# Four PSUM banks for scores and relu, three for maxima, and new matmul orders in an attention kernel

## The chip, the core and the metric

The kernel runs on one core of a Trainium2 chip. The metric is the device time of one execution in microseconds (us); the lower the better. TensorE (PE in the profile; PEld for its weight loads) does the matmuls, VectorE (DVE) and ScalarE (ACT) read their results from the eight banks of PSUM, GpSimd (POOL) and SyncE (SP) do small work and issue DMAs.

## The reference

One input `x` of 2048 rows and 576 columns goes through two attentions of 32 heads with head width 18, and a gate mixes the results. Attention A has keys and values of its own for each head; attention B shares one key and one value head.

```
q, k, v = x @ wqkv                      # A: 32 heads of 18
p = softmax(q k^T * 18**-0.5);  a = (p v) @ wo_A
q = x @ wq;  k = x @ wk;  v = x @ wv    # B: 32 query heads, one k and one v
p = softmax(q k^T * 18**-0.5);  b = (p v) @ wo_B
g = sigmoid((x * gate_w).sum(-1))
out = g * a + (1 - g) * b               # 2048 x 576, float32
```

## The kernel before

A first stage splits `x` and the weights into two parts each and projects them; queries and keys leave as two half-precision parts. Then 64 heads (32 of B, then 32 of A) run one after another, and a last stage finishes the output projection.

A head has 16 steps, one for each 128 keys. A step makes four score matmuls, `sA0` to `sA3` or `sB0` to `sB3` (`step_scores`): 128 keys against 512 queries each, from rows 0 to 55 of the array, into a bank of the pool `ps_s`. ScalarE turns each into exponentials (tile `pt`). Four matmuls with the values then add these to `acc`, a bank of its own (`step_pv`); they run side by side in four column groups of the array, for all 512 columns or for one half of 256.

The softmax needs the row maxima before its exponentials. They are found 22 steps (`LEAD`) ahead of the scores: `step_max` makes matmuls of 128 queries against 512 keys from rows 64 to 117, into a bank of the pool `ps_m`, and VectorE reduces each. In every first step of a pair, one reduction is saved: a matmul with the difference of the first two key blocks (operation `x`) goes through a relu on ScalarE into `xb`, and VectorE adds it to block 0 while it takes the maximum (`mA0`, tile `junk`); block 1 has no matmul of its own. So a pair of steps has eight exponentials and one relu on ScalarE, seven reductions on VectorE, and 16 matmuls `s`, `m` and `x`. Since `s` and `m` use different rows of the array, two of them can run at once.

TensorE takes its matmuls strictly in the written order, and one that waits for its bank holds those behind it. The loop over pairs of steps at the end of the program walks through a string for each pair, and this string is the order:

- `PLAIN` is the ordinary pair.
- `END` comes where a new head begins: the last values of the old head are added (`Q`), then `head_out` copies `acc` to `oe` on VectorE. `AFTER` is the pair behind it.
- `UNIT` is a pair with one unit of the output projection (`U`): 12 matmuls of 288 columns into one more bank of `ps_m`. `SEG` and `at_ends` place the units: one at each start of the heads 33 to 53, one in the middle of every second head from 32 to 52, and in heads 59 to 62 one in nearly every pair.
- `LEADS` and `FIRST` are the pairs before the scores begin and the first with them, `ALONE` those at the end that have no maxima any more.

In the strings, `P` and `Q` stand for the values of a whole step, `p` and `f`, `h` and `H` for the first and second half of one. `max_rows` closes the maxima of a head (once per head, on VectorE). `turn_mask`, `balance` and `shared_v` belong to the first stage; `out_proj` and `last_out` make the output.

Of the kernel before, what the change touches and what calls it, by code (L numbers as in the profile page):

```python
# [8 lines left out]
F32 = mybir.dt.float32  # L9
# [7 lines left out]
PSUM = bass.MemoryType.PSUM  # L17
# [32 lines left out]
def gated_mix_kernel(ctx: ExitStack, tc: tile.TileContext, xT, wall, wv, wo, out):  # L50
# [8 lines left out]
    dram = ctx.enter_context(tc.tile_pool(name="dram", bufs=1, space=DRAM))  # L59
    ps_s = ctx.enter_context(tc.tile_pool(name="ps_s", bufs=3, space=PSUM))  # L60
    ps_m = ctx.enter_context(tc.tile_pool(name="ps_m", bufs=4, space=PSUM))
    ps_o = ctx.enter_context(tc.tile_pool(name="ps_o", bufs=1, space=PSUM))
# [98 lines left out]
    def turn_mask():  # L161
        pt = ps_m.tile([P, 512], F32, name="pm")
        for g in range(4):
            nc.tensor.transpose(pt[:, MT * g:MT * g + MT], mask_r[:, g, :], ident[0:MT, 0:MT])
        nc.vector.tensor_copy(mask, pt[:, 0:4 * MT].rearrange("p (g m) -> p g m", m=MT))
# [28 lines left out]
    def balance(g):  # L194
# [9 lines left out]
        yield  # L204
        pt = ps_m.tile([P, 512], F32, name="pm")
        nc.tensor.transpose(pt[0:2, 0:P], r, ident)
# [5 lines left out]
        yield  # L212
        pb = ps_m.tile([P, 512], F32, name="pm")
        nc.tensor.matmul(pb[:, 0:2], two, dg, start=True, stop=True)
# [60 lines left out]
    def shared_v(c):  # L275
        st = ST.pop(c)
        pv = ps_m.tile([P, 512], F32, name="pm")
# [222 lines left out]

    def step_max(u, i, c, low=False):
# [11 lines left out]
        nc.tensor.matmul(pm, qs[u % 3][b:b + 54, i * P:(i + 1) * P], k, start=True, stop=True)  # L513
        if c == "x":
            MX["x", u, i] = lead.tile([P, 512], F32, name="xb", bufs=2)
            nc.scalar.activation(MX["x", u, i], pm, AF.Relu)  # L516
        elif c == 0 and ("x", u, i) in MX:
            junk = lead.tile([P, 512], BF16, name="junk", bufs=1)
            nc.vector.tensor_tensor_reduce(junk, pm, MX.pop(("x", u, i)), 1.0, -3e38, op0=OP.add, op1=OP.max,  # L519
                                           accum_out=MX[u][:, i, c:c + 1])  # L520
        else:
            nc.vector.tensor_reduce(MX[u][:, i, c:c + 1], pm, axis=AX.X, op=OP.max)  # L522
# [112 lines left out]
    WO = {}  # L635

    def prep_wo(t0, rows):
        nt = len(rows)
# [10 lines left out]
    def out_proj(t0, rows, first=False):  # L649
# [18 lines left out]
        for q in range(8):  # L668
# [3 lines left out]
            for s2 in range(2):  # L672
                st_ = 2 * q + s2
                for hf in range(2):
                    fp = ps_m.tile([P, 512], F32, name="pm")
                    n = 0
# [29 lines left out]
    def last_out():  # L706
# [6 lines left out]
        for j in range(4):  # L713
# [3 lines left out]
            dma(stk[36:54, cs], ol[32 * j:32 * j + 18, :])  # L717
        pt = ps_m.tile([P, 512], F32, name="pm")
        for c in range(4):
# [7 lines left out]
        for st_ in range(16):  # L727
            for hf in range(2):
                ps = ps_m.tile([P, 512], F32, name="pm")
                nc.tensor.matmul(ps[:, 0:288], stk[0:54, st_ * P:st_ * P + P],  # L730
# [60 lines left out]
    FIRST = "sA0 mA2 sA1 mA0 sA2 mA3 mA1 sA3 mB0 sB0 mB1 sB1 mB2 sB2 mB3 sB3 x"  # L791
    PLAIN = "sA0 mA2 sA1 mA0 sA2 mA3 P sA3 mB0 sB0 mB1 sB1 mB2 h sB2 mB3 sB3 x H"
    UNIT = "sA0 mA2 sA1 mA0 sA2 mA3 P sA3 mB0 sB0 mB1 sB1 mB2 U sB2 mB3 sB3 x Q"
    END = "sA0 mA2 sA1 mA3 sA2 mB0 P sA3 mB1 sB0 mA0 sB1 x Q sB2 mB2 sB3 mB3"
    AFTER = "sA0 mA2 p sA1 mA0 sA2 mA3 sA3 x f sB0 mB0 sB1 mB1 h sB2 mB2 sB3 mB3 H"
    ALONE = "sA0 sA1 P U sA2 sA3 U sB0 sB1 h U sB2 sB3 H U"
    LEADS = "V.A mA0 MA1 mA2 MA3 V.B mB0 MB1 mB2 MB3"
    order = None
    for T in range(-LEAD, NSTEP + 2, 2):
# [5 lines left out]
        if M >= 16 and M % 16 == 0 and M // 16 - 1 < NU:  # L805
            max_rows(M // 16 - 1)
        alone = M >= NSTEP
        units = sum(due(t, Tb, Tc, 32) for t in (T, T + 1) for _, _, _, Tb, Tc in SEG)
        order = LEADS if T < 0 else FIRST if T == 0 else ALONE if alone else UNIT if units else \
            END if T % 16 == 0 else AFTER if order is END else PLAIN  # L810
        for op in order.split():
# [8 lines left out]
            elif k in "mM":  # L820
                step_max(*divmod(M + second, 16), int(c), k == "M")
            elif k == "s":
# [10 lines left out]
        if slow and M % 16:  # L833
            for _ in range(2 if T > 1000 else 1):
                if slow:
                    try:
                        next(slow[0])
                    except StopIteration:
                        slow.pop(0)
    while slow:  # L840
        run(slow.pop(0))
# [38 lines left out]
```

## Time and profile before

| | |
|---|---|
| median of 3 runs | 2697.82 us (2697.22 to 2697.87) |
| the profiled execution | 2698.16 us, of which its instructions span 2696.4 us |
| TensorE matmuls busy | 2663.0 us (99%) |
| VectorE busy | 2429.9 us (90%) |
| ScalarE busy | 2389.8 us (89%) |
| mean granted TensorE clock | 0.996 |

Busy shares are averages over stages: the first 280 us or so are projection. Matmuls are pipelined, so a busy TensorE is not one at its peak. In the rows of the timeline, an instruction's start can lie before the end of the one ahead of it on its engine; the distance of two ends then tells the engine's rate.

### The profile page before, as it was taken

Reading aid. Unit: us, or ns where it says so; the run is one execution under the profiler, and the core shown is the slowest. Engines: PE = TensorE matmul, PEld = TensorE weight load, DVE = VectorE, ACT = ScalarE, POOL = GpSimd, SP = SyncE. Lnnn points to the kernel's source line nnn. Section 1 sums busy time; section 2 is a strip of 40 time slices with the busy share of each in tenths; the row PEclk is TensorE's granted clock in tenths of the full one; section 3 lists DMA queues with packets and bytes.
Section 4 is the critical chain, followed back from the end, with each engine's and each line's share of the span. In section 5 each row is a group of like instructions: output and inputs, shape, how many; then the busy total and the mean of one; then the engine's idle time right before and its main releaser. Section 6 shows DMA issues by size and latency. Waiting matters only on the chain.

```text
span 2696.4 us, 57946 instructions
## 1 busy us (share of the span) xinstructions
PE 2663.0 (99%) x22210; PEld 955.2 (35%) x22210; DVE 2429.9 (90%) x4616; ACT 2389.8 (89%) x4809; POOL 280.0 (10%) x520
## 2 busy tenths in 40 slices
PE   9999999999999999999999999999999999999999
PEld 6888322222222222222223333333333332223444
DVE  8347999999999999999999999999999999998865
ACT  4341899999999999999999999999999999998875
POOL 4740000002001100100110001000200011011000
PEclk9999999999999999999999999999999999999998
DMA  6332000011001100110132113112121212122212
GB/s 200 125 110 78 20 20 20 18 32 45 25 20 46 44 20 18 52 33 18 38 76 81 44 48 87 43 49 64 57 67 50 57 51 61 39 73 83 88 36 96
DMA packets 127089, 150.36 MB, mean 56 GB/s; under 512 B 55339, under 2 KB 94411, under 8 KB 125614
## 3 DMA queue, kind: packets, MB, share of 16 engines
q1 hardware_dynamic: 113628, 121.86, 16.0%
q0 software_dynamic: 7968, 19.23, 2.1%
q10 hardware_dynamic: 5216, 5.57, 0.6%
q8 instruction: 174, 2.85, 0.4%
q14 instruction: 103, 0.84, 0.1%
HBM read 90.89 MB, written 46.45 MB: 51 GB/s over the span
## 4 chain that ended last, share of the span: by engine, by line
ACT 51%; PE 40%; DVE 6%; DMA 1%; issue 1%; SPq 1%; DVEq 0%; ACTq 0%
ACT pt L557 45%; PE acc L563 14%; PE ps L550 12%; ACT xb L516 6%; PE pm L679 4%; DVE mx L522 3%; PE pm L243 3%; PE ps L243 3%; PE ps L292 2%; PE pm L513 2%; DVE oe L573 1%; SPq L56 1%; DVE junk L519 1%; DMA xs<-xT 1%; DVE oacc L733 0%
## 5 line engine op out<-in xcount | busy, mean ns | idle before, releaser
L557 ACT ACTIVATE pt<-ps 128x512 f32<-128x512 f32 x4052 | 2095.0, 639 | 69.2 <-PE pm L513 61.2
L522 DVE TENSOR_REDUCE mx<-pm 128x1 f32<-128x512 f32 x3096 | 1941.4, 682 | 89.2 <-PE pm L513 74.9
L550 PE MATMUL ps<-qs,ksb 56*128 56x512 f16 x2688 | 819.4, 380 | 10.6
L513 PE MATMUL pm<-ksb,qs 54*128 54x512 f16 x2364 | 739.7, 383 | 1.9 <-DVE mx L522 1.0
L563 PE MATMUL acc<-pt,vb 128*19 128x512 f32 (+1 forms) x6136 | 592.7, 458 | 1.9
L563 PE MATMUL acc<-pt,vg 128*19 128x256 f32 (+1 forms) x5664 | 579.5, 481 | 2.3 <-DVE oe L573 0.5
L513 PEld LDWEIGHTS <-qs 54*128 54x128 f16 x4096 | 329.9, 93 | 247.3 <-issue 197.1
L550 PE MATMUL ps<-qs,ksa 56*128 56x512 f16 x1364 | 404.4, 379 | 4.8 <-ACT pt L557 1.3
L550 PEld LDWEIGHTS <-ksb 56*128 56x128 f16 x2688 | 175.0, 94 | 623.0 <-issue 576.5
L513 PE MATMUL pm<-ksa,qs 54*128 54x512 f16 x1232 | 385.0, 382 | 0.6 <-ACT xb L516 0.4
L519 DVE CUSTOM_DVE_ANT_0 junk<-pm,xb 128x512 bf16<-128x512 f32 x500 | 340.4, 681 | 0.0
L516 ACT ACTIVATE xb<-pm 128x512 f32<-128x512 f32 x500 | 317.6, 635 | 0.0
L550 PEld LDWEIGHTS <-ksa 56*128 56x128 f16 x1408 | 89.3, 94 | 328.7 <-issue 298.5
L532 POOL TENSOR_SCALAR mt<-mt 128x32 f32<-128x32 f32 x64 | 18.5, 288 | 1612.8 <-DVE mt L530 1612.8
L563 PEld LDWEIGHTS acc<-pt,vb 128*19 128x19 f32 x6136 | 104.0, 97 | 225.6 <-issue 208.5
L563 PEld LDWEIGHTS acc<-pt,vg 128*19 128x19 f32 x5664 | 96.1, 97 | 222.9 <-issue 204.9
L513 PE MATMUL pm<-kdb,qs 54*128 54x512 f16 x372 | 141.7, 381 | 0.0
L573 DVE COPY oe<-acc 128x512 f32<-128x512 f32 x63 | 43.6, 692 | 30.0 <-PE acc L563 27.9
L295 ACT ACTIVATE vst<-ps 128x288 f32<-128x288 f32 x32 | 13.1, 411 | 62.1 <-PE ps L292 62.1
L251 ACT ACTIVATE ph<-ps,tv 128x512 f16<-128x512 f32 x29 | 19.8, 686 | 49.9 <-PE ps L243 34.3
L251 ACT ACTIVATE ph<-pm,tv 128x512 f16<-128x512 f32 x27 | 18.5, 687 | 48.2 <-PE pm L243 35.7
L257 DVE SCALAR_TENSOR_TENSOR pl<-pm,tv,ph 128x512 f16<-128x512 f32 x27 | 20.1, 749 | 37.9 <-ACT ph L251 24.9
(150 smaller groups left out, 1504.1 us busy)
## 6 DMA issues: line engine op xcount, KB each, us to landing
qs<-qkh SPq DMA_DIRECT2D x244, 72.0 KB
qs<-qkl SPq DMA_DIRECT2D x122, 72.0 KB
onh<-oh SPq DMA_DIRECT2D x32, 256.0 KB
onl<-ol SPq DMA_DIRECT2D x32, 256.0 KB
oih<-onh SPq DMA_DIRECT2D x16, 512.0 KB
oil<-onl SPq DMA_DIRECT2D x16, 512.0 KB
ot<-oe SPq DMA_DIRECT2D x220, 36.0 KB
R<-r_d SPq DMA_DIRECT2D x55, 144.0 KB
```

What stands on the lines that cost most here:

```text
L243: nc.tensor.matmul(fp[:, a0:b0], w[a][:kr, k, :], X[b][:kr, k, s0 + a0:s0 + b0], start=(n == 0), stop=(n == len(PROJ) - 1), skip_group_che ...
L251: nc.scalar.activation(h, fp, AF.Copy, scale=t)
L292: nc.tensor.matmul(fp[:, 0:288], X[b][:kr, k, st_ * P:(st_ + 1) * P], w[a][:kr, k, :], start=(n == 0), stop=(n == len(PROJ) - 1))
L513: nc.tensor.matmul(pm, qs[u % 3][b:b + 54, i * P:(i + 1) * P], k, start=True, stop=True)
L516: nc.scalar.activation(MX["x", u, i], pm, AF.Relu)
L519: nc.vector.tensor_tensor_reduce(junk, pm, MX.pop(("x", u, i)), 1.0, -3e38, op0=OP.add, op1=OP.max, accum_out=MX[u][:, i, c:c + 1])
L522: nc.vector.tensor_reduce(MX[u][:, i, c:c + 1], pm, axis=AX.X, op=OP.max)
L550: nc.tensor.matmul(ps, kst(u)[b:b + 56, i * P:(i + 1) * P], qs[u % 3][b:b + 56, c * 512:(c + 1) * 512], start=True, stop=True)
L557: nc.scalar.activation(pt, ps, AF.Exp, scale=SCALE / LIFT ** 2)
L563: nc.tensor.matmul(acc[32 * j:32 * j + 19, a:b], v_of(u, i), PT[u, i, j][:, a:b], start=(i == 0 and a == 0), stop=(i == 15), skip_group_ch ...
L573: nc.vector.tensor_copy(oe, acc)
L679: nc.tensor.matmul(fp[:, 0:288], o[b][:r, t, s2 * P:(s2 + 1) * P], w[a][:r, t, 288 * hf:288 * hf + 288], start=(n == 0), stop=(n == 3 * nt ...
```

## The change

Three things are done at once.

1. `ps_s` has four banks and `ps_m` three, where it was three and four. The matmul `x` that feeds the relu goes to `ps_s`, so that pool serves ScalarE alone in the main stage, and `ps_m` serves VectorE and the units.
2. The strings are new, and there are separate ones for a unit at a head's start (`UNIT_END`) and for the heads 59 on (`UNIT2`). `AFTER` now also follows a head's start with a unit.
3. Where `ps_m` had uses beside the maxima, they are moved: small transposes of the first stage go to parts of `acc`, each fourth maximum of `LEADS` to `ps_s`, and after the loop the output matmuls take turns over both pools (`seven`).

```diff
-    ps_s = ctx.enter_context(tc.tile_pool(name="ps_s", bufs=3, space=PSUM))
-    ps_m = ctx.enter_context(tc.tile_pool(name="ps_m", bufs=4, space=PSUM))
+    ps_s = ctx.enter_context(tc.tile_pool(name="ps_s", bufs=4, space=PSUM))
+    ps_m = ctx.enter_context(tc.tile_pool(name="ps_m", bufs=3, space=PSUM))
...
     def turn_mask():
-        pt = ps_m.tile([P, 512], F32, name="pm")
+        pt = acc[:, 192:256]
...
+    def other():
+        return ps_s.tile([P, 512], F32, name="ps")
+
+    def step_max(u, i, c, low=False, spare=False):
...
-        pm = ps_m.tile([P, 512], F32, name="pm")
+        pm = other() if c == "x" or spare else ps_m.tile([P, 512], F32, name="pm")
...
+    def seven():
+        L["tail"] += 1
+        return other() if L["tail"] % 7 < 4 else ps_m.tile([P, 512], F32, name="pm")
...
-    PLAIN = "sA0 mA2 sA1 mA0 sA2 mA3 P sA3 mB0 sB0 mB1 sB1 mB2 h sB2 mB3 sB3 x H"
+    PLAIN = "mB1 mB3 sA0 sA1 mA3 sA2 P mB2 sA3 x sB0 mA2 sB1 mB0 h sB2 mA0 H sB3"
...
+    UNIT_END = "mB3 sA0 mA2 sA1 mA3 sA2 P sA3 mB1 sB0 mB2 Q x sB1 mA0 sB2 mB0 sB3 U"
...
-        order = LEADS if T < 0 else FIRST if T == 0 else ALONE if alone else UNIT if units else \
-            END if T % 16 == 0 else AFTER if order is END else PLAIN
+        order = LEADS if T < 0 else FIRST if T == 0 else ALONE if alone else (UNIT2 if T >= SEG[1][3] else UNIT_END if T % 16 == 0 else UNIT) if units else \
+            END if T % 16 == 0 else AFTER if T % 16 == 2 and T > 2 else PLAIN
```

What the new strings do to TensorE's queue, at three places. The names: `ps` is a score (in the new kernel also `x`), `pm` a maximum, `acc` the values; `ksb` and `qs` are keys and queries, `kdb` the key difference; the numbers tell tiles apart. First the ordinary pair, from behind `H` to `P`, before:

```order
L550 LDWEIGHTS ksb_95
L550 MATMUL ps_8827<-qs1_93,ksb_95 128x512
L513 LDWEIGHTS qs2_94
L513 MATMUL pm_8831<-ksb_95,qs2_94 128x512
L550 LDWEIGHTS ksb_95
L550 MATMUL ps_8834<-qs1_93,ksb_95 128x512
L513 LDWEIGHTS qs2_94
L513 MATMUL pm_8838<-ksb_95,qs2_94 128x512
L550 LDWEIGHTS ksb_95
L550 MATMUL ps_8842<-qs1_93,ksb_95 128x512
L513 LDWEIGHTS qs2_94
L513 MATMUL pm_8846<-ksb_95,qs2_94 128x512
```

The same stretch of TensorE's queue after the change, from `mB1` to the last matmul ahead of `P`:

```order
L516 LDWEIGHTS qs2_94
L516 MATMUL pm_8788<-ksb_95,qs2_94 128x512
L516 LDWEIGHTS qs2_94
L516 MATMUL pm_8791<-ksb_95,qs2_94 128x512
L553 LDWEIGHTS ksb_95
L553 MATMUL ps_8794<-qs1_93,ksb_95 128x512
L553 LDWEIGHTS ksb_95
L553 MATMUL ps_8798<-qs1_93,ksb_95 128x512
L516 LDWEIGHTS qs2_94
L516 MATMUL pm_8802<-ksb_95,qs2_94 128x512
L553 LDWEIGHTS ksb_95
L553 MATMUL ps_8805<-qs1_93,ksb_95 128x512
```

Where scores and maxima took strict turns, two maxima now follow each other, then two scores, and the last score stands alone before `P`.

Second, TensorE at a head's start (`END`), around the last values of the old head, `Q`, before:

```order
L550 LDWEIGHTS ksb_95
L550 MATMUL ps_9240<-qs2_94,ksb_95 128x512
L513 LDWEIGHTS qs0_92
L513 MATMUL pm_9244<-kdb_96,qs0_92 128x512
L563 MATMUL acc_100<-pt_9159,vb_97 19x512
L563 MATMUL acc_100<-pt_9166,vb_97 19x512
L563 MATMUL acc_100<-pt_9177,vb_97 19x512
L563 MATMUL acc_100<-pt_9184,vb_97 19x512
L550 LDWEIGHTS ksb_95
L550 MATMUL ps_9259<-qs2_94,ksb_95 128x512
L513 LDWEIGHTS qs0_92
L513 MATMUL pm_9263<-ksb_95,qs0_92 128x512
```

And after the change:

```order
L516 LDWEIGHTS qs0_92
L516 MATMUL pm_9282<-ksb_95,qs0_92 128x512
L553 LDWEIGHTS ksb_95
L553 MATMUL ps_9285<-qs2_94,ksb_95 128x512
L553 LDWEIGHTS ksb_95
L553 MATMUL ps_9289<-qs2_94,ksb_95 128x512
L566 MATMUL acc_100<-pt_9193,vb_97 19x512
L566 MATMUL acc_100<-pt_9200,vb_97 19x512
L566 MATMUL acc_100<-pt_9211,vb_97 19x512
L566 MATMUL acc_100<-pt_9223,vb_97 19x512
L553 LDWEIGHTS ksb_95
L553 MATMUL ps_9304<-qs2_94,ksb_95 128x512
```

`Q` has moved behind all maxima of its pair and has one score of the pair left behind it; before, two scores and two maxima came after it.

Third, TensorE around the unit of a head's start (`woh`, `wol` are weights of the output, `oih`, `oil` the normalised heads), before:

```order
L513 MATMUL pm<-ksb,qs_93 128x512
L679 MATMUL pm<-woh,oih 128x288 x4
L679 MATMUL pm<-woh,oil 128x288 x4
L679 MATMUL pm<-wol,oih 128x288 x4
L550 LDWEIGHTS ksa_2749
L550 MATMUL ps<-qs_92,ksa_2749 128x512
```

And after the change:

```order
L553 MATMUL ps<-qs_92,ksa_2740 128x512
L687 MATMUL pm<-woh,oih 128x288 x4
L687 MATMUL pm<-woh,oil 128x288 x4
L687 MATMUL pm<-wol,oih 128x288 x4
L516 LDWEIGHTS qs_93
L516 MATMUL pm<-ksb,qs_93 128x512
```

The unit now stands at the end of its pair, behind all its scores; before, two scores, a maximum, `x` and `Q` followed it.

More of the change, by code (lines that the diff above doesn't have):

```diff
@@ L204, in balance @@
         yield
-        pt = ps_m.tile([P, 512], F32, name="pm")
+        pt = acc[:, 0:P]
         nc.tensor.transpose(pt[0:2, 0:P], r, ident)
@@ L212, in balance @@
         yield
-        pb = ps_m.tile([P, 512], F32, name="pm")
+        pb = acc[:, P:P + 2]
         nc.tensor.matmul(pb[:, 0:2], two, dg, start=True, stop=True)
@@ L276, in shared_v @@
         st = ST.pop(c)
-        pv = ps_m.tile([P, 512], F32, name="pm")
+        pv = acc[:, 256:328]
         for j in range(4):
@@ L499, in gated_mix_kernel @@
     MX = {}
-    def step_max(u, i, c, low=False):
+    def other():
+        return ps_s.tile([P, 512], F32, name="ps")
+    def step_max(u, i, c, low=False, spare=False):
         if u not in MX:
@@ L674, in out_proj @@
                 for hf in range(2):
-                    fp = ps_m.tile([P, 512], F32, name="pm")
+                    fp = seven() if "tail" in L else ps_m.tile([P, 512], F32, name="pm")
                     n = 0
@@ L717, in last_out @@
             dma(stk[36:54, cs], ol[32 * j:32 * j + 18, :])
-        pt = ps_m.tile([P, 512], F32, name="pm")
+        pt = seven()
         for c in range(4):
@@ L728, in last_out @@
             for hf in range(2):
-                ps = ps_m.tile([P, 512], F32, name="pm")
+                ps = seven()
                 nc.tensor.matmul(ps[:, 0:288], stk[0:54, st_ * P:st_ * P + P],
@@ L791, in gated_mix_kernel @@
     FIRST = "sA0 mA2 sA1 mA0 sA2 mA3 mA1 sA3 mB0 sB0 mB1 sB1 mB2 sB2 mB3 sB3 x"
-    PLAIN = "sA0 mA2 sA1 mA0 sA2 mA3 P sA3 mB0 sB0 mB1 sB1 mB2 h sB2 mB3 sB3 x H"
-    UNIT = "sA0 mA2 sA1 mA0 sA2 mA3 P sA3 mB0 sB0 mB1 sB1 mB2 U sB2 mB3 sB3 x Q"
-    END = "sA0 mA2 sA1 mA3 sA2 mB0 P sA3 mB1 sB0 mA0 sB1 x Q sB2 mB2 sB3 mB3"
-    AFTER = "sA0 mA2 p sA1 mA0 sA2 mA3 sA3 x f sB0 mB0 sB1 mB1 h sB2 mB2 sB3 mB3 H"
+    PLAIN = "mB1 mB3 sA0 sA1 mA3 sA2 P mB2 sA3 x sB0 mA2 sB1 mB0 h sB2 mA0 H sB3"
+    UNIT = "mB2 sA0 mB0 sA1 mA0 P mB3 sA2 mA2 sA3 Q mA3 sB0 x sB1 mB1 sB2 U sB3"
+    END = "mA0 sA0 mB0 p mA2 sA1 x mB2 sA2 sA3 mA3 f sB0 mB1 mB3 sB1 sB2 Q sB3"
+    AFTER = "mB3 sA0 mB1 mB2 sA1 p sA2 x sA3 mB0 f mA0 sB0 mA3 sB1 h mA2 sB2 H sB3"
+    UNIT_END = "mB3 sA0 mA2 sA1 mA3 sA2 P sA3 mB1 sB0 mB2 Q x sB1 mA0 sB2 mB0 sB3 U"
+    UNIT2 = "sA0 mA3 sA1 mB0 sA2 P sA3 mB1 sB0 mB2 sB1 x U mA2 sB2 mA0 sB3 Q mB3"
     ALONE = "sA0 sA1 P U sA2 sA3 U sB0 sB1 h U sB2 sB3 H U"
@@ L820, in gated_mix_kernel @@
             elif k in "mM":
-                step_max(*divmod(M + second, 16), int(c), k == "M")
+                step_max(*divmod(M + second, 16), int(c), k == "M", T < 0 and c == "3")
             elif k == "s":
@@ L839, in gated_mix_kernel @@
                         slow.pop(0)
+    L["tail"] = 0
     while slow:
```

## The prediction

> **What bounds the kernel now.** I read the busy times of single heads first (columns: window in us, its length, busy us and instructions of PE, PEld, DVE, ACT, POOL, then TensorE's clock and DMA). The windows are cut at a head's first exponential: a plain head, one with two units, and one of the heads from 59 on.
>
> ```profile
> 677.79:713.65 35.86, 35.51 (x322) 10.07 (x320) 35.17 (x68) 35.49 (x73) 0.74 (x3) 1.00 0.11 33
> 1507.55:1546.13 38.58, 38.36 (x330) 12.64 (x328) 35.46 (x68) 36.60 (x75) 0.75 (x3) 1.00 0.18 46
> 2493.99:2540.58 46.59, 46.53 (x354) 20.00 (x352) 39.02 (x75) 37.40 (x73) 2.83 (x5) 1.00 0.27 87
> ```
>
> In a plain head three engines are full at once, and this row does not say which one sets the pace. The chain of waits does (start, length, what): here one position of two neighbouring heads, then one position of three neighbouring heads with units, then two neighbouring units of the heads from 59 on.
>
> ```profile
> 695.98 3.92 ACT pt L557 x8
> 731.85 3.92 ACT pt L557 x8
> ...
> 1674.78 3.92 ACT pt L557 x8
> 1713.36 3.92 ACT pt L557 x8
> 1750.57 3.92 ACT pt L557 x8
> ...
> 2531.12 1.78 PE pm L679 x12
> 2536.92 1.78 PE pm L679 x12
> ```
>
> Eight exponentials take 3.92 us, 0.49 each. A pair of steps has nine such operations on ScalarE, so it needs 4.41 us and a head of eight pairs 35.28. A plain head takes 35.87; a head with one unit 37.21 and with two 38.58; a late pair, one unit each, 5.80. In plain heads I look for the 0.58 us over ScalarE's floor (35.86 less 35.28). The table of waits has most of it, over 29 heads (318 to 1360 us):
>
> ```profile
> ACT pt L557 <- PE pm L513: 11.4, 36, 0.4
> ```
>
> That is 0.39 us a head (11.4 over 29), about once a head, by up to 0.4: the pair behind `AFTER`. The other 0.19 are gaps too short for the table.
>
> **Prices.** TensorE's timeline over one ordinary pair, from `P` to the next `P` (rows of the maxima that start with a score left out):
>
> ```profile
> 736.14 1.05 PE L563 MATMUL acc<-pt,vb 128*19 128x512 f32 x8
> 737.13 0.39 PE L550 MATMUL ps<-qs,ksb 56*128 56x512 f16 x1
> 737.36 0.38 PE L550 MATMUL ps<-qs,ksb 56*128 56x512 f16 x1
> ...
> 738.10 0.63 PE L563 MATMUL acc<-pt,vb 128*19 128x256 f32 x8
> 738.66 0.39 PE L550 MATMUL ps<-qs,ksb 56*128 56x512 f16 x1
> 738.89 0.38 PE L550 MATMUL ps<-qs,ksb 56*128 56x512 f16 x1
> 739.20 0.63 PE L563 MATMUL acc<-pt,vb 128*19 128x256 f32 x8
> 739.76 0.39 PE L550 MATMUL ps<-qs,ksb 56*128 56x512 f16 x1
> ...
> 740.23 0.37 PE L550 MATMUL ps<-qs,ksb 56*128 56x512 f16 x1
> 740.49 0.37 PE L513 MATMUL pm<-ksb,qs 54*128 54x512 f16 x1
> 740.79 1.06 PE L563 MATMUL acc<-pt,vb 128*19 128x512 f32 x8
> 741.78 0.39 PE L550 MATMUL ps<-qs,ksb 56*128 56x512 f16 x1
> ```
>
> A slot (a score and a maximum side by side) costs 0.22 us. Values of a whole step cost 0.99 (740.79 to 741.78), of a half 0.56 (738.10 to 738.66), and changing over to them adds 0.09 to the slot ahead (738.89 to 739.20 is 0.31). A pair had 8 slots, one whole and two halves: 1.76 + 1.08 + 1.30 = 4.14 us. Now ScalarE and VectorE:
>
> ```profile
> 735.64 0.61 ACT L516 ACTIVATE xb<-pm 128x512 f32<-128x512 f32 x1
> 736.12 4.06 ACT L557 ACTIVATE pt<-ps 128x512 f32<-128x512 f32 x8
> ...
> 742.20 0.60 ACT L557 ACTIVATE pt<-ps 128x512 f32<-128x512 f32 x1
> ...
> 736.75 0.68 DVE L519 CUSTOM_DVE_ANT_0 junk<-pm,xb 128x512 bf16<-128x512 f32 x1
> 737.36 3.67 DVE L522 TENSOR_REDUCE mx<-pm 128x1 f32<-128x512 f32 x6
> 740.95 0.68 DVE L519 CUSTOM_DVE_ANT_0 junk<-pm,xb 128x512 bf16<-128x512 f32 x1
> ...
> 699.86 0.22 DVE L528 TENSOR_REDUCE m<-mx 128x16 f32<-128x64 f32 x1
> 700.32 0.65 DVE L522 TENSOR_REDUCE mx<-pm 128x1 f32<-128x512 f32 x1
> ...
> L573 DVE COPY oe<-acc 128x512 f32<-128x512 f32 x63 | 43.6, 692 | 30.0 <-PE acc L563 27.9
> ```
>
> A score begun at 741.78 reaches ScalarE at 742.20 and is free 0.60 later: 1.02 us. Ends on ScalarE lie 0.49 apart (736.25 to 740.18 for eight). VectorE's seven reductions take 4.20 (736.75 to 740.95), and a head adds 0.46 in `max_rows` (699.86 to 700.32) and 0.61 to 0.69 for the copy: 33.6 + 1.1 = 34.7. A bank of a maximum is held some 0.42 + 0.68 + 0.05 us (the 0.05: the reduce that ended about 740.43 let the maximum start at 740.49).
>
> **The change, part by part.** *Ordinary pairs.* `PLAIN` now needs 9 slots, for `mB0` and `sA2` run alone: 4.36 us on TensorE, still 0.05 under ScalarE's 4.41. With four banks a score waits for the exponential four places ahead. I wrote one period out by hand with `P` at 0: the scores and `x` start at 0.99, 1.21, 1.21, 1.43, 2.51, 3.38, 3.61, 3.83 and 4.04; `sB1` finds its bank 0.2 late, but the lone `mB0` runs in that time, and `mA3` 0.15 late beside the lone `sA2`. Nothing reaches ScalarE. So 4.41 stays: gain 0. VectorE may come 0.28 late before `mB0` holds TensorE.
>
> *Head start.* The same by hand for the old strings gives 0.41 us of idle ScalarE in the pair behind `AFTER`: with three banks the third score behind `P` waits for the exponential three places ahead, `H` comes late, and behind the following `P` the first score is 0.41 late. The table of waits has 0.39, so the method holds. For the new strings, from `H` of the last old pair at 0: last score 0.56, `p` 1.10, `f` 2.68 (`mA3` 0.06 late), `mB3` 3.57 (0.10 late), `Q` 4.09, next score 5.08, whose exponential may end at 6.10 where ScalarE is due at 6.13. VectorE copies `acc` at 5.23, at once behind `mB3`, so `p` of `AFTER` waits 0.14 to 5.97; the last score starts at 9.59 and ends 0.07 late. `max_rows` makes VectorE 0.46 late, of which 0.28 is covered; `mB0` passes on 0.18, and scores are up to 0.14 ahead: 0.045. A plain head loses 0.07 + 0.045 and takes 35.40: gain 0.46. Heads 1 to 31 and 54 to 58 are 36 such: 16.6 us. If VectorE's cover failed, the 1.1 would lie bare (second rival).
>
> *Units.*
>
> ```profile
> 1737.49 1.79 PE pm L679 x12
> L295 ACT ACTIVATE vst<-ps 128x288 f32<-128x288 f32 x32 | 13.1, 411 | 62.1 <-PE ps L292 62.1
> ```
>
> A unit costs TensorE 1.79 + 0.09. `UNIT` and `UNIT2` keep 8 slots, two whole values and the unit: 1.76 + 2.16 + 1.88 = 5.80, which is what late pairs already take; there I count 1 us for heads 59 to 62 (their wait for `oe`). `UNIT_END` and `AFTER` have 17 slots, two whole values, four halves and a unit: 3.74 + 2.16 + 2.60 + 1.88 = 10.38; 0.06 is waited for a score bank and 0.12 for the unit's bank, which ScalarE must empty first (a copy of this shape, 0.41). Less 0.14 by which scores are ahead, that is 10.42, or 1.60 over two ordinary pairs; with 0.045 for `max_rows`, 1.65 where it was 1.93 (37.21 less 35.28): gain 0.28 in 11 heads. A second unit, beside `max_rows`, adds 5.80 + 0.28 of bank waits - 0.14 - 4.41 = 1.53, or 1.48 net of `max_rows`, where it added 1.37: gain 0.17 in 10 heads. Together 4.8, and 0.4 for head 32.
>
> *The rest*, at nothing.
>
> ```profile
> 184.19 9.80 PE pm L243 x42
> ...
> 2671.78 7.62 DVE L687 TENSOR_TENSOR oacc<-pm,oacc 128x288 f32<-128x288 f32 x20
> 2679.32 13.68 DVE L733 SCALAR_TENSOR_TENSOR oacc<-pm,rl,oacc 128x288 f32<-128x288 f32 x32
> ```
>
> The first stage is one chain of matmuls, and a job meets its bank again six jobs later, 9.80 us for each three; the moved transposes are few. At the end VectorE adds without a pause, so seven banks feed it no faster. Without that cover I allow 2 us either way.
>
> **A rule against it.** The rows for a weight load behind a matmul of the same array rows, from the first pair (start, length):
>
> ```profile
> 279.11 0.37 PE L513 MATMUL pm<-ksb,qs 54*128 54x512 f16 x1 [0.21 <-DVE mx L522]
> 279.11 0.09 PEld L513 LDWEIGHTS <-qs 54*128 54x128 f16 x1 [0.50 <-issue]
> ```
>
> Both start at 279.11, so the load runs while its predecessor still streams, and I take a lone slot at 0.22. The Trainium skill (TensorE: Matmul & The Clock Gate, Part 3: Packing small matmuls — row/col tiling) says that weight loads overlap with running matmuls only where the row group differs. By that rule the trace disagrees; if it held, the first rival would be the forecast.
>
> **The rivals.** *Slower: followers on the same rows pay their weight load.* `PLAIN` has two such places (`mB1 mB3`, `sA0 sA1`), the old one none. At 0.09 each TensorE needs 4.36 + 0.18 = 4.54, 0.13 over ScalarE, in some 330 ordinary pairs (36 heads with six, 22 with five or six): +43, less the 22.8 above, 2718. It decides from 0.025 a place. The load row speaks against it; no two such matmuls run freely in this trace. Chance 0.13.
>
> *Three banks for maxima are too few.* If `max_rows` and the copy are passed on to ScalarE for half of their 1.1 us, each head loses 0.55 as it did, and the gain is gone: 2697, no change. For it: VectorE is busy 35.17 of 35.86. Against: seven reductions need only 4.20 of 4.41. Chance 0.13.
>
> *VectorE becomes the bound half way.* If its busy 35.17 is the true need of a head, a plain head ends near 35.6: 9 us there, some 2689 in all. Chance 0.12.
>
> **How the numbers follow.** The terms are 16.6 + 4.8 + 0.4 + 1 = 22.8 us. The profiled execution took 2698.16 (span 2696.4 and 1.8 around it), 0.3 above the median of the runs shown, so 2698.2 - 22.8 = 2675.4; I say 2676. The likeliest case has 0.62 and reaches from 2667 (all of the 0.58 gone in 36 heads is 20.9, units 8, rest 2) to 2687 (half the gain). The range of 8 in 10 goes from 2666 to 2700 and leaves out the slower rival and a little more. About 0.2%, 5.4 us, is what a measurement here can tell from no change. Faster by more than that: 0.62, and most of 0.12: 0.73. Within it: the too few banks and the edge of its neighbour, 0.13. Slower: 0.14, the weight loads and a little unnamed.
>
> **What would show it.** In the profile after: ordinary pairs still 4.41 in the chain, ScalarE's idle time before exponentials in 318 to 1360 us down from 11.4 to 2 or 3, plain heads 35.4 apart, the two pairs at a unit's head start near 10.4, late pairs still 5.8. Wrong, if ordinary pairs take over 4.45 (weight loads), if maxima wait for VectorE and head starts still idle ScalarE by 0.4 (too few banks), or if VectorE has no idle time left.

## The result, and the profile after

The changed kernel takes 2699.76 us (median, 2698.91 to 2701.39), the kernel before 2698.24 beside it: ratio 1.0007, 95% interval 0.9999 to 1.0014. There is no gain. Two of the experiments below (two regions, and max_rows split alone) left a profile at a granted clock of 0.65 and 0.85, so lengths in these two profiles are not compared with others.

The two profiled executions, cut at heads' first exponentials, show where gains and losses lie (lengths in us; the last column is a kernel that comes at the end of the experiments):

| stretch | before | after | difference | four places mended |
|---|---|---|---|---|
| to the start of head 1 | 318.17 | 321.17 | +3.00 | 316.36 |
| heads 1 to 31 | 1114.91 | 1112.02 | -2.89 | 1104.04 |
| heads 32 to 53 (with units) | 834.24 | 832.65 | -1.59 | 828.19 |
| heads 54 to 58 | 180.18 | 179.44 | -0.74 | 178.13 |
| heads 59 to 62 (a unit in each pair) | 185.11 | 187.24 | +2.13 | 185.72 |
| head 63 | 32.12 | 34.23 | +2.11 | 32.05 |
| from the start of the last exponential on | 31.63 | 31.46 | -0.17 | 31.52 |
| span | 2696.35 | 2698.21 | +1.86 | 2676.01 |

First the busy times of single heads of the changed kernel, as in the prediction: a plain head, one with two units, a late one.

```profile
679.56:715.33 35.77, 35.71 (x332) 9.19 (x328) 35.21 (x68) 35.70 (x74) 0.74 (x3) 1.00 0.11 34
1507.52:1546.11 38.59, 38.53 (x337) 11.77 (x336) 35.80 (x68) 36.82 (x75) 0.74 (x3) 1.00 0.17 47
2492.27:2539.31 47.04, 46.95 (x356) 20.09 (x352) 38.86 (x76) 37.81 (x72) 2.82 (x5) 1.00 0.28 87
```

A plain head went from 35.86 to 35.77, a late one from 46.59 to 47.04. The table of waits (321 to 1361 us) and the chain of waits by engine:

```profile
ACT pt L560 <- PE pm L516: 1.9, 8, 0.3
...
PE 84%; DVE 10%; DMA 2%; issue 1%; SPq 1%; ACT 0%; DVEq 0%; POOL 0%; ACTq 0%; POOLq 0%
```

The chain of the kernel before:

```profile
ACT 51%; PE 40%; DVE 6%; DMA 1%; issue 1%; SPq 1%; DVEq 0%; ACTq 0%
```

ScalarE's listed waits fell from 11.4 us to 1.9, as forecast, and the head hardly got shorter. ScalarE's share of the chain fell from 51% to 0%. Where the time went is in the shortest stretches. Windows of one plain head after the change: `END` and `AFTER` together, one ordinary pair, the pair of `max_rows`; and the pair of `max_rows` in a late head.

```profile
715.33:724.59 9.26, 9.20 (x89) 2.50 (x83) 9.26 (x18) 9.16 (x20) 0.00 (x0) 1.00 0.15 41
724.59:728.96 4.37, 4.37 (x42) 1.11 (x40) 4.34 (x9) 4.37 (x10) 0.00 (x0) 1.00 0.02 6
737.72:742.34 4.62, 4.62 (x42) 1.21 (x40) 4.62 (x10) 4.62 (x10) 0.74 (x3) 1.00 0.04 6
2518.69:2524.92 6.23, 6.22 (x46) 2.50 (x45) 5.04 (x12) 5.17 (x11) 0.74 (x3) 1.00 0.02 3
```

The third busy time is VectorE's: 9.26 of 9.26, and 4.62 of 4.62. In these three pairs of a head it has no idle time left. That alone does not show that it sets the pace: in the kernel before, VectorE was also full in the pair in which ScalarE idled, where by the prediction's account scores waited for one of three banks.

```profile
722.49:727.26 4.77, 4.77 (x44) 1.29 (x41) 4.77 (x10) 4.46 (x10) 0.00 (x0) 1.00 0.02 3
```

The ends of ScalarE's operations show where time is lost. They lie 0.49 apart wherever it has work; the places where they lie further apart are its idle gaps. In head 12 these were 0.42 (third pair) and 0.17 (behind `max_rows`) before, 0.59 together. After, they are 0.07 and 0.20 in `END`, 0.11 and 0.03 around `AFTER`, 0.11 and 0.04 behind `max_rows`: 0.56 together. With 72 x 0.49 = 35.28 this is the length of the head, within 0.06. The large gap was replaced by six small ones, most of them below what the table of waits lists.

How the gap of 0.20 arises can be read in `END`, on TensorE (the maximum `mB2`, the score `sA3`, the maximum `mA3`, the values `f`) and on VectorE:

```profile
715.93 0.38 PE L516 MATMUL pm<-ksb,qs 54*128 54x512 f16 x1
716.06 0.38 PE L553 MATMUL ps<-qs,ksb 56*128 56x512 f16 x1
716.43 0.37 PE L516 MATMUL pm<-ksb,qs 54*128 54x512 f16 x1
716.74 0.63 PE L566 MATMUL acc<-pt,vb 128*19 128x256 f32 x8
```

```profile
715.70 0.69 DVE L525 TENSOR_REDUCE mx<-pm 128x1 f32<-128x512 f32 x1
```

`mA3` starts 0.50 us behind `mB2`, where a slot is 0.22. It is the third maximum behind `mB0`, so with three banks it needs the bank of `mB0`, and VectorE's reduction of `mB0` (the last row) ends at 716.39, 0.04 before `mA3` starts. So here a maximum waits 0.28 us for VectorE, and everything behind it in TensorE's order is late with it. A score runs in that time, so the table of waits does not list it.

In the first stage, TensorE of the changed kernel, then of the kernel before:

```profile
39.61 0.58 PE L279 MATMUL acc<-ident,pst 18*128 18x18 f32 x4 [4.17 <-ACT ph L251]
40.12 2.08 PE L243 MATMUL ps<-xh,wh 128*128 128x512 f32 x4
42.00 1.91 PE L243 MATMUL ps<-xh,wl 128*128 128x512 f32 x4
```

```profile
35.82 0.39 PE L279 MATMUL pm<-ident,pst 18*128 18x18 f32 x4 [0.54 <-DVE pd L260]
36.14 1.20 PE L243 MATMUL ps<-xh,wh 128*128 128x512 f32 x4
37.18 1.10 PE L243 MATMUL ps<-xh,wl 128*128 128x512 f32 x4
```

The second set of transposes in `shared_v` idles TensorE for 4.17 us where it was 0.54, and the matmuls behind it then take 1.91 for four instead of 1.10. The row names ScalarE as the one that ended the wait; VectorE's copy of the first set, from the same place in `acc`, ends then too (39.46).

### The profile page after: what moved, and what is told of

It is laid out like the page before. It is cut to its first block, busy times and chain, and to the rows that moved or that the text cites. A ratio compares the mean times of both kernels' runs of the same rounds, so it can differ in the third digit from the quotient of the medians.

```text
span 2698.2 us, 59414 instructions
## 1 busy us (share of the span) xinstructions
PE 2673.8 (99%) x22674; PEld 908.9 (34%) x22674; DVE 2439.5 (90%) x4616; ACT 2404.1 (89%) x4809; POOL 279.9 (10%) x520
## 4 chain that ended last, share of the span: by engine, by line
PE 84%; DVE 10%; DMA 2%; issue 1%; SPq 1%; ACT 0%; DVEq 0%; POOL 0%; ACTq 0%; POOLq 0%
PE acc L566 34%; PE ps L553 20%; PE pm L516 14%; DVE mx L525 6%; PE pm L687 4%; PE pm L243 3%; PE ps L243 3%; PE ps L516 3%; PE ps L292 2%; DVE junk L522 1%; DVE oe L576 1%; SPq L56 1%; DMA R<-r_d 1%; DMA xs<-xT 1%; DVE oacc L741 0%
## 5 line engine op out<-in xcount | busy, mean ns | idle before, releaser
L525 DVE TENSOR_REDUCE mx<-pm 128x1 f32<-128x512 f32 x3074 | 1920.6, 683 | 71.2 <-PE pm L516 34.5
L516 PE MATMUL pm<-ksb,qs 54*128 54x512 f16 x2342 | 769.4, 381 | 3.2 <-DVE mx L525 2.0
L516 PEld LDWEIGHTS <-qs 54*128 54x128 f16 x4096 | 291.7, 94 | 597.4 <-issue 532.6
L516 PE MATMUL pm<-ksa,qs 54*128 54x512 f16 x1232 | 400.8, 380 | 1.2 <-DVE mx L525 0.3
L553 PEld LDWEIGHTS <-ksb 56*128 56x128 f16 x2688 | 198.5, 94 | 405.5 <-issue 374.4
L519 ACT ACTIVATE xb<-ps 128x512 f32<-128x512 f32 x500 | 309.7, 619 | 7.3 <-PE ps L553 7.3
L553 PEld LDWEIGHTS <-ksa 56*128 56x128 f16 x1408 | 100.0, 94 | 203.3 <-issue 186.6
L516 PE MATMUL ps<-kdb,qs 54*128 54x512 f16 x372 | 140.9, 379 | 0.0
L695 DVE TENSOR_TENSOR oacc<-pm,oacc 128x288 f32<-128x288 f32 x53 | 23.4, 457 | 42.7 <-PE pm L687 42.7
```

The lines of the kernel that those rows point to most:

```text
L553: nc.tensor.matmul(ps, kst(u)[b:b + 56, i * P:(i + 1) * P], qs[u % 3][b:b + 56, c * 512:(c + 1) * 512], start=True, stop=True)
```

## The experiments

### Which part does what: banks or strings

All strings of before in the new banks:

```diff
-    PLAIN = "mB1 mB3 sA0 sA1 mA3 sA2 P mB2 sA3 x sB0 mA2 sB1 mB0 h sB2 mA0 H sB3"
+    PLAIN = "sA0 mA2 sA1 mA0 sA2 mA3 P sA3 mB0 sB0 mB1 sB1 mB2 h sB2 mB3 sB3 x H"
```

> Edit: the changed kernel with all strings of before, and with their rules of which pair takes which; four banks for scores and relu, three for maxima stay. Theory A (the banks alone already end ScalarE's wait of 0.4 us at a head start, and the old strings leave TensorE a reserve of 0.27 us in an ordinary pair, which covers what VectorE makes late): plain heads under 35.7, the time under 2698. Theory B (three banks for maxima are too few for the old strings, whose maxima stand in tight turns): maxima wait for VectorE in every pair, plain heads over 36, the time over 2710. My own sum for A, 0.3 us a head from the wait that goes: plain heads 35.55, 2688 to 2692 with the late heads as before.

Measured: 2742.36 us, ratio 1.0166 (1.0151 to 1.0181). Theory B. One plain head and one late head:

```profile
682.90:719.05 36.15, 35.84 (x322) 8.36 (x320) 35.42 (x68) 35.49 (x73) 0.75 (x3) 1.00 0.10 33
2525.22:2576.03 50.81, 48.94 (x354) 19.43 (x352) 39.00 (x75) 37.39 (x73) 2.82 (x5) 1.00 0.26 80
```

The new banks cost the old strings 0.29 us in a plain head and 4.2 in a late one. Their gaps in a plain head grew to 0.61 behind `AFTER` and 0.26 behind `max_rows`.

The new strings in the old banks:

```diff
-    ps_s = ctx.enter_context(tc.tile_pool(name="ps_s", bufs=4, space=PSUM))
-    ps_m = ctx.enter_context(tc.tile_pool(name="ps_m", bufs=3, space=PSUM))
+    ps_s = ctx.enter_context(tc.tile_pool(name="ps_s", bufs=3, space=PSUM))
+    ps_m = ctx.enter_context(tc.tile_pool(name="ps_m", bufs=4, space=PSUM))
```

> Edit: the changed kernel with three banks for scores and four for maxima and relu, as before; the new strings stay. Theory A (the new strings need the fourth score bank: sA0 sA1 and the score behind P find their bank in use): ordinary pairs take longer than 4.41, by 0.1 to 0.3 us, in some 450 pairs, so 2740 to 2830. Theory B (the strings carry the change alone, and the fourth bank for maxima takes away VectorE's lateness at head starts): plain heads under 35.6, the time under 2695.

Measured: 2853.86 us, ratio 1.0579 (1.0561 to 1.0596). Theory A, and above its range: ordinary pairs take 4.84, a plain head 38.46. So neither half of the change stands alone; the new strings make three banks bearable, and need the fourth score bank.

### What sets the pace

```diff
-            MX["x", u, i] = lead.tile([P, 512], F32, name="xb", bufs=2)
-            nc.scalar.activation(MX["x", u, i], pm, AF.Relu)
+            if "xb" not in MX:
+                MX["xb"] = lead.tile([P, 512], F32, name="xb", bufs=1)
+                nc.scalar.activation(MX["xb"], pm, AF.Relu)
+            MX["x", u, i] = MX["xb"]
```

> Edit: the changed kernel, but the relu on ScalarE is done once in the whole program and its first result is used in all later pairs (this leaves out the relu of each pair; the matmul x stays). ScalarE then has 64 operations in a head, 31.4 us, instead of 72, 35.28. Theory A (TensorE's sum is a bound of its own: six ordinary pairs of nine slots at 4.36 and two at 4.58, 35.3 us): plain heads take 35.2 to 35.5, so the reserve of ScalarE only takes away the idle gaps, 0.3 to 0.5 us a head, about 2680. Theory B (ScalarE alone sets the pace and TensorE would follow): plain heads fall to 34 or less, 2640 or less. Theory C (VectorE's lateness sets the head, not ScalarE at all): heads stay at 35.77, 2700.

Measured: 2694.62 us, ratio 0.9989 (0.9979 to 0.9998). One plain head:

```profile
678.15:713.83 35.68, 35.62 (x336) 9.21 (x328) 35.27 (x68) 33.30 (x65) 0.75 (x3) 1.00 0.11 34
```

ScalarE has 3.9 us less to do in a head (eight of 0.49), and the head is 0.09 shorter. That is between A and C. Pair by pair, the ordinary ones stay at 4.36, TensorE's sum for nine slots; `END` (4.73) and `AFTER` (4.51) stay as they were, and the pair of `max_rows` takes 4.65. ScalarE, with idle time now in every pair, sets neither the ordinary pairs nor the slow ones. In the changed kernel its own sum (4.41), TensorE's (4.36) and VectorE's (4.20) lie so close that taking one away frees almost nothing.

### The pair of max_rows

```diff
-            max_rows(M // 16 - 1)
+            max_reduce(M // 16 - 1)
+        if M > 16 and M % 16 == 2 and M // 16 - 1 < NU:
+            max_rows(M // 16 - 1)
```

Here `max_reduce` is the first reduction of `max_rows`, and `max_rows` keeps the rest.

> Edit: the changed kernel with max_rows in two halves: its reduction at the pair where it stood, its transposition, the work on GpSimd and the transfers one pair later. Theory A (VectorE has 0.17 us to spare in an ordinary pair, seven reductions of 0.6 in 4.37, so 0.46 in one pair comes through to TensorE, while 0.22 and 0.2 in two pairs come through for less than half): the pair of max_rows falls from 4.62 to 4.45, its neighbour rises by less than 0.05; ScalarE's idle time of 0.148 us a head falls to about 0.05; 0.1 us in some 55 heads and 0.2 to 0.4 in four late ones, about 2693. Theory B (a three-bank ring passes any lateness on in full): the two halves cost together what they cost as one, 2700.

Measured: 2687.52 us, ratio 0.9964 (0.9949 to 0.9979), 12.2 us under the changed kernel. Theory A, and by more than the 7 us expected: the whole 0.148 us of idle time behind `max_rows` is gone, as the kernel of four mended places shows (its pair of `max_rows` takes 4.41 instead of 4.62):

```profile
729.84:734.25 4.41, 4.41 (x43) 1.11 (x40) 4.41 (x11) 4.41 (x10) 0.00 (x0) 1.00 0.00 0
```

The same in the kernel before:

> Edit: the kernel before with max_rows split over two pairs, nothing else. Theory A (what split max_rows gave has to do with three banks and with a TensorE without reserve, so the change itself made max_rows dearer): the kernel before, with a reserve of 0.27 us in a pair and four banks, has only its idle gap of 0.169 us a head to lose, and gains at most 0.12 in 55 heads and nothing in the late ones, 2691 to 2695. Theory B (the split is worth the same in both kernels, 12 us): 2685, and the change would then be worth nothing beside it.

Measured: 2689.64 us, ratio 0.997 (0.9957 to 0.9982): 8.4 us less, between the two theories and nearer to A. In plain heads both kernels lost about the same (0.169 before, 0.148 after) and both get it back. Four banks and a reserve of 0.27 us on TensorE had not covered `max_rows` either. Where the pair also has a unit, the change made it dearer: in a late head (60) that pair is 5.81 before, 6.23 after and 5.94 when split, and in head 40 it is 5.71, 6.12 and 5.88.

### The head start

Two scratch tiles, because two fused reductions (those that add the relu's result while they take the maximum) meet there on VectorE, `mA0` at the end of `PLAIN` and `mA0` at the start of `END`:

```diff
-            junk = lead.tile([P, 512], BF16, name="junk", bufs=1)
+            junk = lead.tile([P, 512], BF16, name="junk", bufs=2)
```

> Edit: the changed kernel with two scratch tiles junk where there was one. At a head start two fused reductions with junk follow each other on VectorE, and 0.26 us lie between them and the reduce ahead. Theory A (the second waits for the end of the first, because both write the one scratch): the 0.26 goes at each head start, maxima behind it are no longer late, and plain heads take 35.5 instead of 35.77; 0.2 to 0.27 us a head over some 58 heads is 12 to 16 us, about 2685. Theory B (it waits for its matmul's semaphore, which comes no earlier): heads stay at 35.77, the time at 2700. Theory C (the wait goes, but ScalarE's or TensorE's next wait takes its place): the gap on VectorE closes and heads shrink by less than 0.1, 2695 or more.

Measured: 2696.22 us, ratio 0.9993 (0.9984 to 1.0003), some 3.5 us under the changed kernel; a plain head takes 35.67. Between A and C. VectorE's timeline at the place, in the changed kernel and with two tiles:

```profile
714.82 0.08 DVE L522 DVE_READ_ACCUMULATOR2_ANT mx<- 128x1 f32 x1
715.08 0.69 DVE L522 CUSTOM_DVE_ANT_0 junk<-pm,xb 128x512 bf16<-128x512 f32 x1 [0.17 <-PE pm L516]
```

```profile
715.16 0.08 DVE L522 DVE_READ_ACCUMULATOR2_ANT mx<- 128x1 f32 x1
715.30 0.69 DVE L522 CUSTOM_DVE_ANT_0 junk<-pm,xb 128x512 bf16<-128x512 f32 x1
```

The second reduction starts 0.26 us behind the first one's reading with one tile and 0.14 with two. The tile is 0.12 of it; the other 0.14 stays, and no run shows why. ScalarE's gap behind `Q` falls by as much, from 0.20 to 0.085.

`END` with two whole values (the string of `UNIT_END` without its unit):

```diff
-    END = "mA0 sA0 mB0 p mA2 sA1 x mB2 sA2 sA3 mA3 f sB0 mB1 mB3 sB1 sB2 Q sB3"
+    END = "mB3 sA0 mA2 sA1 mA3 sA2 P sA3 mB1 sB0 mB2 Q x sB1 mA0 sB2 mB0 sB3"
```

> Edit: the changed kernel with one string replaced: END is the string of UNIT_END without the unit, so the values come as two wholes, P and Q, where they were two halves and a whole. By TensorE's prices END falls from 4.58 us (10 slots at 0.22, two halves at 0.65, a whole at 1.08) to 3.92 (8 slots, two wholes). Theory A (the head start of the changed kernel is set by TensorE's own sum, 4.58 in END and 4.58 in AFTER, measured 4.73 and 4.51): the two pairs take 8.7 to 8.85 together instead of 9.24, ScalarE's idle time at a head start falls from 0.41 to 0.1, a plain head takes 35.3 to 35.4, and 36 such heads give 13 to 16 us, about 2685. Theory B (behind the whole Q at the middle of the pair ScalarE runs dry, as it did in the kernel before by 0.42): the idle time only moves, plain heads stay within 0.1 of 35.77, 2697 to 2702.

Measured: 2711.04 us, ratio 1.0049 (1.0033 to 1.0065): worse than B. ScalarE in that pair:

```profile
718.52 2.14 ACT L560 ACTIVATE pt<-ps 128x512 f32<-128x512 f32 x4
721.00 0.60 ACT L519 ACTIVATE xb<-ps 128x512 f32<-128x512 f32 x1 [0.35 <-PE ps L553]
```

With two scores between `P` and `Q` it runs dry by 0.46 us. `END` takes 4.93, and a plain head 36.07. TensorE's sum of slots, which had fallen by 0.66, did not decide.

The four places of the sections here (split, scratch, and the two edits of the next section) were then put into one kernel, and three variants of it tried. With four scores between `P` and `Q`:

> Edit: the kernel of the four mended places with another string END: sA0 mA2 sA1 mA3 sA2 mB0 P sA3 mB1 sB0 mA0 sB1 x sB2 mB2 mB3 Q sB3. It has two whole values, 4.14 us by TensorE's prices instead of 4.58, but with all four scores of the second step and the relu between P and Q where the earlier trial with two wholes had two scores. Theory A (that trial failed only because two scores are too few to carry ScalarE over Q): ScalarE's idle time at a head start falls from about 0.29 us to under 0.1, END and AFTER take 8.85 to 8.95 together instead of 9.15, and 36 heads give 7 to 10 us against the run beside it. Theory B (two whole values in one pair run ScalarE dry wherever they stand, or VectorE's copy of acc, now with every maximum ahead of it, comes too late for p): no gain or a loss of up to 10 us.

Measured: 2681.88 us where the kernel without it took 2677.83. Theory B: `END` and `AFTER` take 9.25 instead of 9.15, because the copy of `acc` now comes after all maxima and `p` waits for it:

```profile
714.45 0.63 PE L566 MATMUL acc<-pt,vb 128*19 128x256 f32 x8 [0.16 <-DVE oe L576]
```

The score ahead of `p` starts at 713.91, 0.54 before it; in the kernel beside it this distance is 0.44 (711.92 to 712.36). The difference is the 0.10.

With the ordinary pair of before:

> Edit: the kernel of the four mended places with the ordinary pair of before (PLAIN with 8 slots, 4.14 us on TensorE) in place of the new one with 9 slots and 4.36. Theory A (TensorE at 4.36 has no reserve, so every lateness of VectorE stays in the head; with 0.22 us a pair in reserve it would be made up): the gaps behind head starts shrink and a head takes 0.1 to 0.2 less, 6 to 12 us less than the run beside it. Theory B (the old order of maxima waits for three banks in each pair, which eats the reserve, as its run with all old strings hints, where the pair of max_rows cost 4.78): heads take 0.1 to 0.3 more, 6 to 17 us more.

Measured: 2703.14 us, 25 more, beyond B: a plain head takes 36.16, and `END` alone 5.26. The old pair ends with `x`, the new `END` begins with the maximum that needs its relu, and VectorE waits:

```profile
714.21 0.69 DVE L522 CUSTOM_DVE_ANT_0 junk<-pm,xb 128x512 bf16<-128x512 f32 x1 [0.63 <-ACT xb L519]
```

VectorE loses 0.63 us there, and the head 0.63 against the run beside it (36.16 and 35.53). TensorE's reserve of 0.22 in each pair made up for none of it. So VectorE's lateness comes through in full at this place.

With two half values left out at each plain head start (the edit also takes the one in `AFTER` from heads that start with a unit):

```diff
+            elif k == "f" and order is END:
+                for j in range(4):
+                    del PT[(*divmod(T - 2, 16), j)]
-            elif T >= 2:
+            elif T >= 2 and not (k == "h" and order is AFTER):
```

> Edit: the kernel of the four mended places with two half values left out at each plain head start: f in END and h in AFTER (this leaves a part of the sum of values out; 0.65 us each of TensorE's time). Theory A (what ScalarE still idles at a head start, 0.29 us, is TensorE's own sum: 4.58 in END and 4.58 in AFTER, against 8.82 for the 18 operations on ScalarE): with 1.30 us less on TensorE the idle time falls under 0.1, END and AFTER take 8.8 to 8.9 together instead of 9.15, a plain head 35.2 to 35.35, and the whole 7 to 11 us less than 2677.8. Theory B (it is the wait of p for the copy of acc, or the change from values to scores, which need banks and a first exponential that waits): 0.15 to 0.29 us of idle time stay, a plain head takes 35.4 or more, the whole 2673 or more.

Measured: 2673.12 us, 4.7 less, of which 2.1 lie in the heads 32 to 53; a plain head takes 35.45, and 0.21 of the 0.29 us of idle time stays. These are the numbers of theory B. `END` and `AFTER` together, with all values (first row) and with 1.3 us of them left out:

```profile
707.77:716.90 9.13, 9.07 (x89) 2.40 (x83) 9.13 (x18) 9.13 (x19) 0.00 (x0) 1.00 0.14 41
```

```profile
707.91:716.85 8.94, 8.53 (x73) 2.40 (x67) 8.94 (x18) 8.94 (x20) 0.00 (x0) 1.00 0.16 43
```

TensorE's busy time falls by 0.54 and the stretch by 0.19, of which the next pair gives 0.13 back (4.50 instead of 4.37). VectorE is full in both. The wait has only changed its name. In the table of waits over some 29 heads, maxima hardly wait for VectorE in the changed kernel (first row) and not at all in the one with four mends; here they do, once a head (second row):

```profile
PE pm L516 <- DVE mx L525: 0.2, 1, 0.2
```

```profile
PE pm L516 <- DVE mx L525: 6.8, 30, 0.2
```

VectorE's own sum says the same: 14 reductions at 0.60 and the copy at 0.61 are 9.01, with the 0.14 between the two fused ones 9.15, against 8.82 for 18 operations on ScalarE. The difference, 0.33, is about the 0.29 of idle time. TensorE's own sum, 9.16, is as large, but with 1.3 less of it most of the idle time stayed. That agrees with the 0.63 us of the run before. It was not tried directly, by taking the copy away, and `p` still waits for the copy in this run too.

### The first stage and the last head

Two regions of `acc` for the shared values:

```diff
-        pv = acc[:, 256:328]
+        pv = acc[:, 256 + 72 * (c % 2):328 + 72 * (c % 2)]
```

> Edit: the changed kernel, but the transposes of the shared values take turns over two regions of acc by the column block. Theory A (the one region makes the second set of transposes wait 4.17 us on TensorE for VectorE's copy of the first, and the idle time is followed by matmuls at half clock): that wait is gone, the first maximum of the leading steps comes 4 to 5 us earlier than 209.2 us, the first exponential about 3.5 us earlier than 281.3, and the whole kernel takes some 3 us less than the changed one, about 2697. Theory B (VectorE is late in the first stage for another reason, or all of acc is tracked as one tile, so that a region makes no difference): the wait stays at 4 us and the time at 2700.

Measured: 2700.31 us, ratio 1.0009 (0.9999 to 1.0019). No gain, as theory B has it. In its profile, too, the second set of transposes starts only behind the end of the copy of the first (43.59 and 43.44 us; 39.61 and 39.46 in the changed kernel), and its row names this copy, so the two regions did not part them. That all of `acc` is tracked as one tile would explain it, and is not shown.

All small transposes back in `ps_m`, and one score of a step, not two, in `ps_m` in head 63:

```diff
-        pv = acc[:, 256:328]
+        pv = ps_m.tile([P, 512], F32, name="pm")
...
-        ps = (ps_m if alone and c < 2 else ps_s).tile([P, 512], F32, name="pm" if alone and c < 2 else "ps")
+        ps = (ps_m if alone and c < 1 else ps_s).tile([P, 512], F32, name="pm" if alone and c < 1 else "ps")
```

> Edit: the changed kernel with two parts undone or mended that lie far from each other and are read apart. (1) The small transposes of the first stage (mask, balance, shared values) go to banks of ps_m again and not to parts of acc. Theory A (their regions of acc make TensorE wait for VectorE's copies): the first maximum of the leading steps comes 4 to 5 us earlier than 209.2 us and the first exponential about 3.5 us earlier than 281.3. Theory B (three banks for maxima in the leading steps, or the order of banks in the first stage, cost the time): both stay within 1 us. (2) In the last head only the first score of a step, not two, goes to ps_m. Theory A (the units of the last pairs wait there for banks, because VectorE's additions hold one of only three): the last two pairs take 4.4 and 4.7 us instead of 5.57 and 5.66, 2 us less. Theory B (ScalarE or the additions themselves set them): no change. With both A the whole takes 2694; with both B 2700.

Measured: 2697.34 us, 2.4 under the changed kernel. The last head: theory A, 32.05 instead of 34.23. The first stage: theory B, the first exponential is at 281.6, and the stall is there under another name:

```profile
37.19 0.39 PE L279 MATMUL pm<-ident,pst 18*128 18x18 f32 x4 [4.35 <-DVE pd L260]
```

TensorE waits there for VectorE to empty a bank of `ps_m`; by the theory of the next run, three projections hold all three. With `pv` in a bank of `ps_s`, and the three mends above:

```diff
-        pv = acc[:, 256:328]
+        pv = ps_s.tile([P, 512], F32, name="ps")
```

> Edit: the changed kernel with four places mended at once, which are read apart by their place: max_rows split over two pairs, two scratch tiles junk, one score of a step in ps_m in the last head, and (new) the transposes of the shared values in a bank of ps_s, whose fourth bank is free in the first stage. What the single runs gave adds up to 12.2 + 3.5 + 2.2. Theory A (the first stage loses its 4 us because the second set of transposes finds no free place: in acc the one region, in ps_m the three banks that three projections hold): the 4.5 us wait of TensorE near 40 us is gone, the first exponential comes at 278 and not at 281.3, and the whole takes 2678 to 2680. Theory B (something else sets the first stage): first exponential at 281 again, 2682. In plain heads the pair of max_rows takes 4.45 instead of 4.62, END 4.64, a head 35.5.

Measured: 2677.83 us, ratio 0.9925 (0.9913 to 0.9938): the fastest complete kernel here, 20.2 us under before. Theory A; the second set of transposes no longer waits, and the first exponential comes at 276.7:

```profile
35.31 0.42 PE L279 MATMUL ps<-ident,pst 18*128 18x18 f32 x4
```

Against the kernel before with `max_rows` split (2689.64), 11.8 us remain to the change and its other mends.

## Why the prediction was wrong

The forecast was 2676 with 22.8 us of gain; the time is 2699.8, at the very edge of the stated range (2666 to 2700). The span was to fall by 22.8 us and rose by 1.86. The table above splits these 24.7: 13.0 in plain heads, 3.6 in heads with units, 3.1 in late heads, 3.0 in the first stage, 2.1 in head 63, less 0.2 at the end. Two of the forecast's signs came (ordinary pairs as before, listed waits down to 1.9), and so did two of its signs of being wrong: maxima wait for VectorE while head starts idle ScalarE by 0.4, and VectorE has no idle time left there.

**Ordinary pairs: right.** Forecast: no gain, nine slots at 4.36 just under ScalarE's 4.41. They start 4.36 to 4.41 apart and have no gap.

**The weight loads: rightly set aside.** Followers on the same rows would have made the pair 4.54; it is 4.37. So the trace disagrees once more with the rule of the Trainium skill (TensorE: Matmul & The Clock Gate, Part 3) that a weight load overlaps only with matmuls of other row groups.

**Head start: the term of 0.07 us was mis-sized; it is 0.41.** The old gap of 0.42 did go. But the step that lets `f` start at 2.68 with "`mA3` 0.06 late" took VectorE's reductions to follow each other without a pause; `mA3` is 0.28 late. In the trace (`H` at 713.83) `f` starts at 2.91, `Q` at 4.34 instead of 4.09 and the next score at 5.33 instead of 5.08: all are 0.23 to 0.25 late, because VectorE had lost 0.26 between two fused reductions, which the sum does not have. So the exponential that was to end 0.03 before it was due ended about 0.2 behind. With two scratch tiles VectorE loses 0.12 less there, and `f` starts at 2.78. The rest is VectorE's sum over these two pairs: 9.0 us without any gap, more than ScalarE's 8.82.

**max_rows: the term of 0.045 is 0.148.** I counted 0.28 of VectorE's 0.46 as covered and scores as up to 0.14 ahead. Split in two, it costs a plain head nothing; as one piece, it came through by a third.

**The cover that failed.** Both terms rest on "33.6 + 1.1 = 34.7" for VectorE in a head of 35.28: enough on the whole. Three banks hold half a pair of maxima, so this reserve is not carried from pair to pair; it must hold in each. That is the rival "three banks for maxima are too few": half of 1.1 us lost in each head, 0.55, was its price, and 0.56 is the measured idle time. I gave it 0.13. That the two numbers meet is partly chance, for 0.12 of the 0.56 comes from the scratch tile, which the rival does not have. And its name is only half of the cause, since with four banks `max_rows` cost a head no less (0.17).

**Units, late heads and head 63.** Heads with one unit gained 0.13 instead of 0.28, heads with two nothing instead of 0.17. In head 39 the two pairs at the start take 10.55 where 10.42 was foretold, and the pair of `max_rows` 4.62 again; in head 40 the pair that has `max_rows` and the second unit takes 6.12 where 5.94 was counted (5.88 when `max_rows` is split). "I count 1 us" for heads 59 to 62 became a loss of 2.1, most of it in the pair of `max_rows` (6.23 where it was 5.81, in head 60). Why `max_rows` costs more beside a unit, no run shows. Head 63 was not priced at all; its units and two scores of each step shared the three banks.

**The rest, "at nothing".** That "the moved transposes are few" was true and irrelevant: one set of four stopped TensorE for 4.2 us. I counted their work and not the copy that a set in the same place waits for.

## What to carry to other kernels

When three engines are all within 2% of the bound, add up each engine's work pair by pair, or whatever stretch its buffers can hold, and not over a whole period: a reserve elsewhere in the period could not be used here. A wait that disappears from the table of waits may only have been cut into pieces below its threshold; compare the distance of ends on the engine that should be full. Two short pieces of work in a row on the full engine are worth separating by a pair: splitting `max_rows` gave 12 us here, and the whole change nothing.

## What was not expected of the hardware

After the 4.17 us without matmuls in the first stage, the granted clock is half for 6 us. Windows of the changed kernel and, for the same time, of the kernel before:

```profile
39.60:45.70 6.10, 6.09 (x17) 4.91 (x18) 5.35 (x10) 2.90 (x5) 4.09 (x7) 0.50 0.39 129
```

```profile
39.60:45.70 6.10, 5.75 (x27) 4.10 (x25) 5.66 (x10) 4.03 (x7) 4.49 (x8) 1.00 0.46 154
```

The column behind POOL is the clock, 0.50 and 1.00. The Trainium skill (TensorE: Matmul & The Clock Gate, Part 1) says that TensorE falls to half its clock after an idle window of about 3.4 us. This trace agrees: 4.17 us of idle time did it, and 0.54 did not. So a stall there costs its length and some more: this one is 3.6 us longer than that of before, and the first maximum comes 5.0 us later (209.2 and 204.2).
